# The last batch's second product as seven block products, with one block sum made by two accumulating DMAs

## The chip, the core and the metric

The kernel runs on one core of one Trainium2 chip. Its time is the device time of one execution in microseconds, taken as the median of several runs. The profile is one further execution with the hardware profiler on; its span runs from the first to the last instruction and is shorter than the device time of that execution.

## What is computed

Two stages. The first is attention between 512 tokens and 32 states of each of 8 batches and 8 heads, in both directions; the second takes the result, rearranged to 8 x 544 rows of 512, through a two-layer net. Softmax is along the last axis.

```python
# x: (8, 8, 512, 64)   state: (8, 8, 32, 64)   scale = 1 / 8
a     = softmax(scale * x @ state.T)      # tokens read states
xread = a @ state
a2    = softmax(scale * state @ x.T)      # states read tokens
sread = a2 @ x
X = concat([xread, sread], tokens)        # -> (8 * 544, 512)
h = X @ w_in                              # w_in (512, 2048)
g = s * relu(h) ** 2 + b
return g @ w_out                          # w_out (2048, 512), result float32
```

## The kernel before

**The two layers.** `w_in` and `w_out` stay in SBUF as fp16 (`w_out16`: four tiles of four row blocks). For tokens the state's values are folded into `w_in` first (`at_M`: M = state @ w_in for each head), so that layer one of a batch is M times the attention weights A (`layer1_x`, 16 blocks f of 128 hidden units for 512 tokens). ScalarE takes the relu from PSUM into `r` (two f to a tile, five tiles), VectorE squares two f at a time into the batch's tile `g` of [128, 16 f, 512 tokens] (`square`, L397). The factor s and the bias b leave the hidden layer: s is applied at the end, and b becomes a row `bias_bc` that is added at the end.

**Layer two.** `layer2(tag, rr, q)` (L423) is a quarter of the sum over f for 128 tokens: four matmuls, each with a 128 x 128 block of g as the loaded operand and `w_out_f(f)` of 512 columns streaming past it, into one PSUM bank. There are two such banks (`ps_o`, tag `po`). After four quarters `store` (L435) makes s * ops + bias in one VectorE instruction (L437) and sends the 128 rows out by DMAs on SP's queue (L441).

**The order.** It is written by hand; each engine works through its own queue in the order of the program. `phase(tag, before, behind)` (L573) runs 16 steps. A step issues the pieces due before it, then layer one of block i of the next batch, then at even steps the square of the blocks i-2 and i-1, then the pieces due behind. Batch b's phase runs layer one of batch b+1 beside layer two of batch b, from `l2(b)`: one quarter in each step. Attention for later batches, its loads on GpSimd's queue (`load_x`, `load_xn`) and the products M lie in the same steps. The last phase has the tag `sr`: layer one of the 256 state rows of all batches (`layer1_sr`, four matmuls of 256 columns in each step) beside layer two of batch 7. Layer two of the state rows follows it, in two blocks of 128 rows, the second in two column halves (L702, L706, L709).

Of the kernel before, what the change touches and what calls it, by code (L numbers as in the profile page):

```python
# [10 lines left out]
FP32 = mybir.dt.float32  # L11
FP16 = mybir.dt.float16
# [3 lines left out]
def kernel(  # L16
# [12 lines left out]
    nc = tc.nc  # L29
    AF = mybir.ActivationFunctionType  # L30
    ALU = mybir.AluOpType
    AX = mybir.AxisListType

    B, H, S, D = x.shape
    Ns = state.shape[2]
    DM = H * D
    DF = moe_w_in.shape[1]
    P = 128
    NK = DM // P
    NKF = DF // P  # L40
    NG = H // 4
    SCH = S // P
# [4 lines left out]
    HALF = S // 2  # L47
    scale = float(1.0 / np.sqrt(D))

    out_BSn = out.rearrange("(bb st) n -> bb st n", bb=B)  # L50

    konst = ctx.enter_context(tc.tile_pool(name="konst", bufs=1))
    wpool = ctx.enter_context(tc.tile_pool(name="wpool", bufs=1))
# [6 lines left out]
    opool = ctx.enter_context(tc.tile_pool(name="opool", bufs=4))  # L60
# [3 lines left out]
    ps_o = ctx.enter_context(tc.tile_pool(name="ps_o", bufs=2, space=bass.MemoryType.PSUM))  # L64
    ctx.enter_context(tc.manual_schedule())

    def two_banks(name, dtype=FP32, own=False):

        pool, tag = (ps_t, "pt") if own else (ps_a, "pa")
        return pool.tile([P, 2, 2048 // mybir.dt.size(dtype)], dtype, name=name, tag=tag)  # L70

    def mm(out, lhsT, rhs, start=True, stop=True, tp=None, is_transpose=None):
        skip = out.offset * mybir.dt.size(out.dtype) >= 2048
        return nc.tensor.matmul(  # L74
            out, lhsT, rhs, start=start, stop=stop, tile_position=tp,
            is_transpose=is_transpose, skip_group_check=skip,
        )
# [21 lines left out]
    s_bc, b_bc = sb_bc[:, 0:1], sb_bc[:, 1:2]  # L99
# [3 lines left out]
    bias_bc = konst.tile([P, DM], FP32, name="bias_bc")  # L103
    srdT = konst.tile([P, NK, Ns, B], FP16, name="srdT")
    w_in16 = [wpool.tile([P, NK, 512], FP16, name=f"w_in16_{j}") for j in range(NJ)]
    w_out16 = [wpool.tile([P, 4, DM], FP16, name=f"w_out16_{q}") for q in range(NKF // 4)]


    xh_t, xn_t = {}, {}
# [1 line left out]
    def load_x(b):  # L111

        if b > 2:
            nc.gpsimd.tensor_copy(ahead, at[b - 1]["xT"][0:1, 0, 0])  # L114
        xh_t[b] = xpool.tile([P, NG, NT, D], FP16, name=f"xh_{b}", tag="xh")
        for g in range(NG if b else 1):
            nc.gpsimd.dma_start(  # L117
                out=xh_t[b][:, g].rearrange("p j d -> p (j d)"),
                in_=x[b, 4 * g : 4 * g + 4].rearrange("r (t j) d -> (r t) (j d)", j=NT),
            )  # L120

    def load_xn(b):

        xn_t[b] = xpool.tile([P, H, SCH, D], FP16, name=f"xn_{b}", tag="xn")
        for jh in range(4):
            nc.gpsimd.dma_start(  # L126
                out=xn_t[b][32 * jh : 32 * jh + 32].rearrange("t h c d -> t h (c d)"),
                in_=x[b].rearrange("h (t jh c) d -> jh t h (c d)", t=32, jh=4)[jh],
            )
# [5 lines left out]

    def load_w_out(q):
        nc.gpsimd.dma_start(
            w_out16[q], moe_w_out.rearrange("(q f p) n -> q p f n", p=P, f=4)[q]
        )

    rows = state.rearrange("b (g r) n d -> (r n) (b g) d", g=NG)
# [12 lines left out]
    load_w_in(1)  # L154
    load_x(1)
    load_w_out(0)
    load_w_in(2)
    load_w_out(1)
# [7 lines left out]
        return w_in16[f // 4][:, k, P * (f % 4) : P * (f % 4) + P]  # L166

    def w_out_f(f):
        return w_out16[f // 4][:, f % 4, :]


    def place(h):
# [24 lines left out]
    def pair_states(i0, i1):  # L197
        nc.vector.transpose(
            stE[:, i0:i1].rearrange("p i n e -> p (i n e)").bitcast(FP32),
            stn[:, i0:i1].rearrange("p i d -> p (i d)").bitcast(FP32),  # L200
        )
# [26 lines left out]
    def at_xT(b, g=None, p=None):  # L228

        if "xT" not in at[b]:  # L230
            keep = b < 3
            at[b]["xT"] = (konst if keep else apool).tile(
                [P, NG, S, 2], FP16, name=f"xT_{b}", tag=f"xTk{b}" if keep else "xT"
            )
        out = at[b]["xT"].rearrange("p g s e -> p g (s e)").bitcast(FP32)
        in_ = xh_t[b].rearrange("p g j d -> p g (j d)").bitcast(FP32)
        nc.vector.transpose(part(out, p, g), part(in_, p, g))  # L237
# [141 lines left out]
    G_t, R_t = {}, {}  # L379
# [43 lines left out]
    def layer2(tag, rr, q):  # L423
        if q == 0:
            ops_t[tag, rr] = ps_o.tile([P, DM], FP32, name=f"ops_{tag}_{rr}", tag="po")
        for f in range(4 * q, 4 * q + 4):
            nc.tensor.matmul(  # L427
                ops_t[tag, rr],
                G_t[tag][:, f, P * rr : P * rr + P],
                w_out_f(f),  # L430
                start=(f == 0),
                stop=(f == NKF - 1),
            )

    def store(tag, rr, rows, n=1):  # L435
        osb = opool.tile([P, DM], FP32, name=f"osb_{tag}_{rr}", tag="osb")
        nc.vector.scalar_tensor_tensor(  # L437
            osb, ops_t.pop((tag, rr)), s_bc, bias_bc, ALU.mult, ALU.add
        )
        for i in range(n):  # L440
            nc.sync.dma_start(rows[i], osb[P // n * i : P // n * i + P // n])  # L441

    def out_x(b, rr):
        rows = out_BSn[b, 0:S]
        if b:
            store(b, rr, rows.rearrange("(t r i e) n -> r i t e n", r=SCH, i=2, e=2)[rr], 2)
        else:
            store(b, rr, [rows.rearrange("(t r j) n -> r j t n", r=SCH, j=4)[rr]])

    def spread_scalars():  # L450
        sps = two_banks("sbps")[:, 0, 0:2]
        mm(sps, ones32, sb_one)
        act(sb_bc, sps)
# [174 lines left out]
    def first():  # L628

        out = []  # L630
        units = [(rr, 3) for rr in (0, 1)]
        units += [(rr, q) for rr in (2, 3) for q in range(4)]
        out += [(1, bias_all)]
        for n, (rr, q) in enumerate(units):
            step = n + n // 2
            out += [(step, lambda rr=rr, q=q: layer2(0, rr, q))]
            if q == 3:
                out += [(step + 1, lambda rr=rr: out_x(0, rr))]
        return out

    def l2(b, lead=0):

        out = []
        for i in range(NKF):
            step = max(0, (i - lead) * NKF // (NKF - lead))
            if i and i % 4 == 0:
                out += [(step, lambda i=i: out_x(b, i // 4 - 1))]
            out += [(step, lambda i=i: layer2(b, i // 4, i % 4))]
        return out[:lead], out[lead:]

    left = []
    for b in range(0, B):
        before, behind = l2(b, 3 if b == 1 else 0) if b else ([], first())
        behind = left + behind
        if b + 3 < B:
            before += [(2 if b else 5, lambda b=b: load_x(b + 3))]
        if b + 3 < B:
            before += [(13, lambda b=b: at_xT(b + 3))]
        if b and b + 2 < B:
            before += [(7, lambda b=b: load_xn(b + 2))]  # L660
        if b == B - 3:
            before += [(9, lambda: load_xn(0))]
        if b == B - 2:
            before += [(4, lambda: load_xn(1)), (7, lambda: load_xn(2))]
        if b == 0:
            before += [(4, lambda: pair_states(4, NR)), (3, lambda: turn_states(4, 12, act)), (4, lambda: turn_states(12, NR, act))]
        if b + 2 < B:
            s = (1, 2, 3, 3, 4, 4, 5, 6, 7, 8, 9) if b else (5, 6, 7, 8, 9, 8, 9, 10, 11, 12, 13)
            before += [] if b else [(3, lambda: at_xT(2))]
            before += chain(b + 2, s)  # L670
            if b:
                before += [(7, lambda b=b: at_a2(b + 2))]
                before += [(10, lambda b=b: at_a2T(b + 2, dve))]
        if b > 1 and b + 1 < B:
            before += [(3 if b == B - 2 else 1, lambda b=b: at_V(b + 1))]
        if b:
            plan = [(6 if b < B - 2 else 0, 1, [(b + 1, 3), (b + 2, 0)][: B - 1 - b])]
            plan += [(12, 1, [(b + 2, 1), (b + 2, 2)])] if b + 2 < B else []
            plan += [(1, 1, [(2, 2)])] if b == 1 else []
        else:  # L680
            plan = [(2, 0, [(1, 3)]), (10, 0, [(2, 0), (2, 1)])]
        for step, own, units in plan:
            make, copies, left = pieces(step, own, *units)
            before, behind = before + make, behind + copies
        if b == B - 2:
            before += late(0, (1, 2, 3, 4, 5, 6, 7)) + late(1, (5, 6, 7, 7, 8, 9, 10))
            before += late(2, (8, 9, 10, 11, 12, 13, 15))
        phase(b + 1 if b + 1 < B else "sr", before, behind)
        if b:
            out_x(b, 3)  # L690


# [6 lines left out]
    for part in range(2):  # L699
        sl = slice(DM // 2 * part, DM // 2 * part + DM // 2)  # L700
        for f in range(NKF):
            nc.tensor.matmul(  # L702
                ops[:, sl], G_t["sr"][:, f, P:], w_out_f(f)[:, sl],
                start=(f == 0), stop=(f == NKF - 1),
# [35 lines left out]
```

## Time and profile before

| | us |
|---|---|
| time, median of 3 runs (lowest to highest) | 233.09 (233.02 to 233.31) |
| the profiled execution, own time | 233.29 |
| its span | 231.5 |
| last phase (`sr`), first matmul to the first of the state rows' layer two | 198.85 to 219.65 |
| one square, 128 x 1024 fp16 (L397), mean | 0.683 |
| one eviction of a layer-two bank (L437), mean | 0.745 |
| a store of 128 KB on SP (L441), issue to landing, median | 2.6 |
| a load xn of 128 KB on GpSimd's queue (L126), issue to landing, median | 6.1 |
| granted TensorE clock, mean over the span | 0.989 |

How to read it: the chain of waits goes back from the last instruction to what released each step. The order of time lists instructions with their start and length, merged where alike, and in square brackets how long the engine had stood idle before them and what ended it. The answer by stretches gives busy time and, in brackets, number of instructions for each engine, then the granted clock, the share of the DMA engines' time and GB/s. PE is TensorE, PEld its loading of weights, DVE VectorE, ACT ScalarE, POOL GpSimd, SP the engine that issues stores.

### The profile page before, as it was taken

How to read it: one execution, taken by the hardware profiler on the slowest of the kernel's cores; microseconds unless marked ns; L12 is line 12 of the kernel's file. 1: busy time of each engine (PE TensorE's matmuls, PEld its weight loads, DVE VectorE, ACT ScalarE, POOL GpSimd, SP SyncE). 2: the span in 40 equal slices, each digit the busy share in tenths (PEclk: the TensorE clock that was granted, in tenths of full speed). 3: DMA queues.
4: the chain of work that ended last, by engine and by line, in shares of the span. 5: the costliest groups of instructions: out<-in, count | busy, mean ns of one | idle time of the engine just before them, and what ended most of it. 6: DMA issues, size and time to landing. Idle time of an engine off the chain costs nothing.

```text
span 231.5 us, 4326 instructions
## 1 busy us (share of the span) xinstructions
PE 219.7 (95%) x1735; PEld 101.7 (44%) x1735; DVE 164.0 (71%) x251; ACT 130.5 (56%) x247; POOL 34.7 (15%) x65
## 2 busy tenths in 40 slices
PE   6687999999999999999999999999999999999993
PEld 2143334344444444444444444444434444665552
DVE  2887998788997699759884988498736686422330
ACT  2285676583886568646855685568477445323200
POOL 8431001006002300320025200030003120000000
PEclk9799999999999999999999999999999999999998
DMA  7999990625932960494149923182223782132222
GB/s 168 197 204 207 208 127 14 149 68 86 171 64 53 127 121 19 99 134 91 41 93 135 186 47 76 44 111 45 56 43 61 117 139 45 31 64 46 47 60 76
DMA packets 22920, 22.40 MB, mean 97 GB/s; under 512 B 4084, under 2 KB 16628, under 8 KB 22900
## 3 DMA queue, kind: packets, MB, share of 16 engines
q0 software_dynamic: 16640, 12.52, 37.3%
q1 hardware_dynamic: 5584, 9.44, 16.7%
q8 instruction: 13, 0.21, 0.3%
q10 hardware_dynamic: 676, 0.16, 0.3%
q14 instruction: 7, 0.06, 0.1%
HBM read 25.72 MB, written 8.91 MB: 150 GB/s over the span
## 4 chain that ended last, share of the span: by engine, by line
PE 84%; DMA 7%; DVE 3%; ACT 2%; POOL 2%; issue 1%; ACTq 0%; POOLq 0%
PE ops L427 45%; PE hps L389 22%; DMA w_in<-in_moe_w_in_dram 7%; PE mps L74 4%; PE hps_sr L389 3%; PE T L74 3%; PE vps L74 2%; PE ops_sr L702 2%; PE aps L74 2%; PE ops_sr L427 1%; POOL xh L117 1%; POOL w_in L132 1%; ACT E L316 1%; DVE g L416 1%; DVE U L257 1%
## 5 line engine op out<-in xcount | busy, mean ns | idle before, releaser
L427 PE MATMUL ops<-w_out,g 128*128 128x512 f16 x512 | 130.7, 379 | 0.7 <-DMA w_out<-in_moe_w_out_dram 0.7
L392 ACT ACTIVATE r<-hps 128x512 f16<-128x512 f32 x120 | 70.7, 600 | 48.1 <-PE hps L389 47.6
L427 PEld LDWEIGHTS <-g 128*128 128x128 f16 x512 | 50.0, 98 | 57.5 <-issue 0.9
L389 PE MATMUL hps<-A,M 128*128 128x512 f16 x240 | 70.1, 380 | 0.2 <-ACT r L392 0.2
L397 DVE TENSOR_TENSOR g<-r 128x1024 f16<-128x1024 f16 x60 | 40.9, 683 | 17.2 <-ACT r L392 17.0
L389 PEld LDWEIGHTS <-M 128*128 128x128 f16 x240 | 20.6, 97 | 27.9 <-issue 8.0
L372 ACT CAST M<-mps 128x512 f16<-128x512 f32 x50 | 29.4, 587 | 0.0
L126 POOL DMA_DIRECT2D xn<-in_x_dram x32 | 18.4, 585 | 54.5 <-PE vps L74 53.5
L437 DVE SCALAR_TENSOR_TENSOR osb<-ops,sb_bc,bias_bc 128x512 f32<-128x512 f32 x32 | 23.8, 745 | 1.1 <-PE ops L427 1.0
L316 ACT ACTIVATE E<-T,nms 128x512 f16<-128x512 f32 x16 | 11.0, 687 | 7.7 <-DVE nms L311 7.7
L392 ACT ACTIVATE r_sr<-hps_sr 128x256 f16<-128x256 f32 x16 | 6.1, 384 | 14.4 <-PE hps_sr L389 14.4
L114 POOL COPY ahead<-xT 1x2 f16<-1x2 f16 x5 | 0.9, 174 | 88.9 <-DVE xT L237 88.9
L274 ACT ACTIVATE E<-Dm 128x1024 f16<-128x1024 f32 (+1 forms) x9 | 8.7, 962 | 9.7 <-DVE Dm L267 9.6
L397 DVE TENSOR_TENSOR g_sr<-r_sr 128x512 f16<-128x512 f16 x8 | 3.4, 424 | 13.9 <-ACT r_sr L392 13.9
L257 DVE STREAM_TRANSPOSE U<-T 128x1024 f32<-128x1024 f32 (+1 forms) x9 | 10.9, 1207 | 3.0 <-PE T L74 3.0
L74 PE MATMUL mps<-w_in,stT 64*32 64x512 f16 x256 | 11.1, 388 | 1.3 <-DMA w_in<-in_moe_w_in_dram 1.3
L279 DVE TENSOR_REDUCE z<-E 128x32 f32<-128x1024 f16 (+1 forms) x9 | 9.9, 1100 | 2.8 <-ACT E L274 2.6
L354 DVE CAST srdT<-vps 128x128 f16<-128x128 f32 x8 | 5.8, 728 | 7.4 <-PE vps L74 7.4
L237 DVE STREAM_TRANSPOSE xT<-xh 128x1024 f32<-128x1024 f32 (+2 forms) x12 | 10.2, 870 | 1.0 <-DMA xh<-in_x_dram 1.0
L308 DVE TENSOR_REDUCE nm<-T 128x2 f32<-128x1024 f32 x8 | 9.7, 1214 | 1.2 <-PE T L74 1.2
L74 PE MATMUL T<-xT,stE 32*32 32x512 f16 (+1 forms) x192 | 7.5, 380 | 2.7 <-DVE xT L237 2.4
L267 DVE TENSOR_TENSOR Dm<-U,mu 128x1024 f32<-128x1024 f32 (+1 forms) x9 | 9.9, 1098 | 0.1
(59 smaller groups left out, 159.8 us busy)
## 6 DMA issues: line engine op xcount, KB each, us to landing
out_dram<-osb SPq DMA_DIRECT2D x56, 128.0 KB, 2.6
xn<-in_x_dram POOLq DMA_DIRECT2D x32, 128.0 KB, 6.1
xh<-in_x_dram POOLq DMA_DIRECT2D x15, 256.0 KB, 5.0
w_in<-in_moe_w_in_dram POOLq DMA_DIRECT2D x4, 512.0 KB, 12.5
w_out<-in_moe_w_out_dram POOLq DMA_DIRECT2D x4, 512.0 KB, 17.7
out_dram<-osb SPq DMA_DIRECT2D x4, 256.0 KB
xf<-in_x_dram SPq DMA_DIRECT2D x1, 512.0 KB, 3.5
out_dram<-osb_sr SPq DMA_DIRECT2D x1, 256.0 KB, 2.8
```

The source lines that it names most:

```text
L74: return nc.tensor.matmul(out, lhsT, rhs, start=start, stop=stop, tile_position=tp, is_transpose=is_transpose, skip_group_check=skip,)
L126: nc.gpsimd.dma_start(out=xn_t[b][32 * jh : 32 * jh + 32].rearrange("t h c d -> t h (c d)"), in_=x[b].rearrange("h (t jh c) d -> jh t h (c ...
L237: nc.vector.transpose(part(out, p, g), part(in_, p, g))
L257: nc.vector.transpose(part(U, p, g), part(at[b]["T"], p, g))
L267: nc.vector.tensor_tensor(blk(part(Dm, p, g)), blk(part(at[b]["U"], p, g)), over_n(part(at[b]["mu"], p, g)), ALU.subtract,)
L316: nc.scalar.activation(E2[:, g], at[b]["T"][:, g], AF.Exp, bias=at[b]["nms"][:, g : g + 1], scale=scale, accum_out=rs[:, g : g + 1],)
L372: nc.scalar.copy(at[b]["M"][:, g, 512 * j : 512 * j + 512], at[b]["mps", j][:, g, :])
L389: nc.tensor.matmul(hps, lhsT, rhs, start=(i == 0), stop=(i == len(terms) - 1))
L392: nc.scalar.activation(R_t[tag, f - f % 2][:, f % 2], hps, AF.Relu)
L397: nc.vector.tensor_mul(new_G(tag, r.shape[2])[:, f : f + 2], r, r)
L427: nc.tensor.matmul(ops_t[tag, rr], G_t[tag][:, f, P * rr : P * rr + P], w_out_f(f), start=(f == 0), stop=(f == NKF - 1),)
L437: nc.vector.scalar_tensor_tensor(osb, ops_t.pop((tag, rr)), s_bc, bias_bc, ALU.mult, ALU.add)
```

## The change

Layer two of batch 7 is a product of 512 tokens x 2048 hidden units with 2048 x 512 weights. It is cut into 2 x 2 blocks: A(i, j) is token half i and the even (j = 0) or odd (j = 1) blocks f of g, B(j, n) the same f and column half n of `w_out`. `fast_layer2` makes the four blocks of the result from seven products by Winograd's form of Strassen's scheme:

- sums of g: S1 = A10 + A11, S2 = S1 - A00, S3 = A00 - A10, S4 = A01 - S2;
- sums of the weights: T1 = B01 - B00, T2 = B11 - T1, T3 = B11 - B01, T4 = B10 - T2;
- products in this order: X = A00·B00, Y = A01·B10, X += S2·T2, W = S1·T1, X += S3·T3, W += S4·B11, X += A11·T4, with evictions of X, Y and W in between that put the four result blocks together in SBUF.

Each product is made in two units h (the blocks f below 8, and the others) of eight matmuls of 256 columns. Units 0 to 7 are due at steps 0 to 7, units 8 to 13 at steps 9 to 14. Each sum of g is made in two halves too. S3 gets a tile of its own. S2 and S4 are written by VectorE over A00 and A01. S1 is written over A10, once S3 has read it, by a DMA from SBUF to SBUF on GpSimd's queue that adds A11 to it (`s1`): two DMAs of 128 partitions x 4 rows of 256 fp16. X, Y and W are PSUM tiles of the tag `po`; Y and W follow one another.

The eight halves of weight sums are subtractions on VectorE at steps 14 and 15 of the phases of batches 2 to 5. `w_out16` becomes one tile. The results of batch 7 gather in two tiles `osx` and leave in eight DMAs, four at step 13 and four at step 15, in place of two after every fourth step.

```diff
+    def weight_sum(name, h):
+        if name not in fast_w:
+            fast_w[name] = konst.tile([P, NKF // 2, HALF], FP16, name=f"w_{name}")
...
+        nc.vector.tensor_sub(T[name], a, b)
+
+    def fast_layer2(b):
+        G = G_t[b]
+        S3 = konst.tile([P, NKF // 2, HALF], FP16, name="S3")
...
+        def A(i, j, h=None):
+            k0, k1 = (0, NKF // 2) if h is None else (4 * h, 4 * h + 4)
+            return G[:, 2 * k0 + j : 2 * k1 : 2, HALF * i : HALF * i + HALF]
...
+        def s3(h):
+            add(S3[:, 4 * h : 4 * h + 4], A(0, 0, h), A(1, 0, h), ALU.subtract)
+        def s1(h):
+            nc.gpsimd.dma_start(out=A(1, 0, h), in_=A(1, 1, h), accum_op=ALU.add)
+        def s2(h):
+            add(A(0, 0, h), A(1, 0, h), A(0, 0, h), ALU.subtract)
+        def s4(h):
+            add(A(0, 1, h), A(0, 1, h), A(0, 0, h), ALU.subtract)
...
+        products = [
+            ("X", A(0, 0), orig(0, 0), True, False),
+            ("Y", A(0, 1), orig(1, 0), True, True),
+            ("X", A(0, 0), summed("T2"), False, False),
+            ("W", A(1, 0), summed("T1"), True, False),
+            ("X", S3, summed("T3"), False, False),
+            ("W", A(0, 1), orig(1, 1), False, True),
+            ("X", A(1, 1), summed("T4"), False, True),
+        ]
+        out = [(u + u // 8, lambda u=u: product(*products[u // 2], u % 2)) for u in range(14)]
+        out += [(1, lambda: evict(top, 0, "X"))]
+        for h in range(2):
+            out += [(h, lambda h=h: s3(h)), (h, lambda h=h: s1(h))]
+            out += [(2 + h, lambda h=h: s2(h)), (4 + h, lambda h=h: s4(h))]
+        out += [
+            (3, lambda: evict(top, 0, "Y", True)),
+            (5, lambda: evict(top, 1, "X")),
+            (7, lambda: evict(low, 1, "W")),
+            (10, lambda: evict(low, 1, "X", True)),
+            (12, lambda: evict(top, 1, "W", True)),
+            (13, lambda: put(0, 0)), (13, lambda: put(0, 1)),
+            (15, lambda: evict(low, 0, "X")),
+            (15, lambda: put(1, 0)), (15, lambda: put(1, 1)),
+        ]
+        return out
...
-        before, behind = l2(b, 3 if b == 1 else 0) if b else ([], first())
+        if b == B - 1:
+            before, behind = [], fast_layer2(b)
+        else:
+            before, behind = l2(b, 3 if b == 1 else 0) if b else ([], first())
+        if 1 < b < 6:
+            name = f"T{b - 1}"
+            before += [(14 + h, lambda h=h, name=name: weight_sum(name, h)) for h in range(2)]
...
-        if b:
+        if b and b < B - 1:
             out_x(b, 3)
```

More of the change, by code (lines that the diff above doesn't have):

```diff
@@ L70, in two_banks, with mm @@
         return pool.tile([P, 2, 2048 // mybir.dt.size(dtype)], dtype, name=name, tag=tag)
-    def mm(out, lhsT, rhs, start=True, stop=True, tp=None, is_transpose=None):
-        skip = out.offset * mybir.dt.size(out.dtype) >= 2048
+    def mm(out, lhsT, rhs, start=True, stop=True, tp=None, is_transpose=None, skip=False):
+        skip = skip or out.offset * mybir.dt.size(out.dtype) >= 2048
         return nc.tensor.matmul(
@@ L105 @@
     w_in16 = [wpool.tile([P, NK, 512], FP16, name=f"w_in16_{j}") for j in range(NJ)]
-    w_out16 = [wpool.tile([P, 4, DM], FP16, name=f"w_out16_{q}") for q in range(NKF // 4)]
+    w_out16 = wpool.tile([P, NKF, DM], FP16, name="w_out16")
     xh_t, xn_t = {}, {}
@@ L137, in load_w_out @@
         nc.gpsimd.dma_start(
-            w_out16[q], moe_w_out.rearrange("(q f p) n -> q p f n", p=P, f=4)[q]
+            w_out16[:, 4 * q : 4 * q + 4], moe_w_out.rearrange("(q f p) n -> q p f n", p=P, f=4)[q]
         )
@@ L168, in w_out_f @@
     def w_out_f(f):
-        return w_out16[f // 4][:, f % 4, :]
+        return w_out16[:, f, :]
     def place(h):
@@ L448, in out_x @@
             store(b, rr, [rows.rearrange("(t r j) n -> r j t n", r=SCH, j=4)[rr]])
+    fast_w = {}
+    def weight_sum(name, h):
+        if name not in fast_w:
+            fast_w[name] = konst.tile([P, NKF // 2, HALF], FP16, name=f"w_{name}")
+        w = w_out16[:, 8 * h : 8 * h + 8]
+        B = [[w[:, k::2, HALF * n : HALF * n + HALF] for n in range(2)] for k in range(2)]
+        T = {k: t[:, 4 * h : 4 * h + 4] for k, t in fast_w.items()}
+        a, b = {
+            "T1": lambda: (B[0][1], B[0][0]),
+            "T2": lambda: (B[1][1], T["T1"]),
+            "T3": lambda: (B[1][1], B[0][1]),
+            "T4": lambda: (B[1][0], T["T2"]),
+        }[name]()
+        nc.vector.tensor_sub(T[name], a, b)
@@ new lines, in fast_layer2, with add, product, orig @@
+    def fast_layer2(b):
+        G = G_t[b]
+        S3 = konst.tile([P, NKF // 2, HALF], FP16, name="S3")
+        top, low = (opool.tile([P, 2, DM], FP32, name=f"osx_{b}_{i}", tag=f"osx{i}", bufs=1) for i in range(2))
+        ps = {}
+        def A(i, j, h=None):
+            k0, k1 = (0, NKF // 2) if h is None else (4 * h, 4 * h + 4)
+            return G[:, 2 * k0 + j : 2 * k1 : 2, HALF * i : HALF * i + HALF]
+        def add(out, x, y, op):
+            nc.vector.tensor_tensor(out, x, y, op)
+        def s3(h):
[6 more added lines that the diff above has]
+            add(A(0, 1, h), A(0, 1, h), A(0, 0, h), ALU.subtract)
+        def product(bank, lhs, rhs, first, last, h):
+            if first and h == 0:
+                ps[bank] = ps_o.tile([P, 2, HALF], FP32, name=f"opf_{b}_{bank}", tag="po")
+            for k in range(4 * h, 4 * h + 4):
+                for rr in range(2):
+                    mm(
+                        ps[bank][:, rr], lhs[:, k, P * rr : P * rr + P], rhs(k),
+                        start=(first and k == 0 and rr == 0), stop=(last and k == NKF // 2 - 1 and rr == 1), skip=True,
+                    )
+        def orig(j, n):
+            return lambda k: w_out_f(2 * k + j)[:, HALF * n : HALF * n + HALF]
+        def summed(name):
+            return lambda k: fast_w[name][:, k]
+        def evict(out, n, bank, plus=None):
+            out = out[:, :, HALF * n : HALF * n + HALF]
+            bias = bias_bc[:, HALF * n : HALF * n + HALF].unsqueeze(1).to_broadcast([P, 2, HALF])
+            nc.vector.scalar_tensor_tensor(
+                out, ps[bank], s_bc, bias if plus is None else out, ALU.mult, ALU.add
+            )
+        def put(i, rr):
+            t = (top, low)[i][:, rr]
+            rows = out_BSn[b, 0:S].rearrange("(t r i e) n -> r i t e n", r=SCH, i=2, e=2)[2 * i + rr]
+            for n in range(2):
+                nc.sync.dma_start(rows[n], t[64 * n : 64 * n + 64])
+        products = [
[23 more added lines that the diff above has]
+        return out
```

## The prediction

> **What bounds the kernel now.** I read the page first (busy shares, the chain that ended last, the costliest groups), then the order of time around the place of the change, then that stretch's busy time by engine, then the DMA rows. The page:
>
> ```profile
> span 231.5 us, 4326 instructions
> PE 219.7 (95%) x1735; PEld 101.7 (44%) x1735; DVE 164.0 (71%) x251; ACT 130.5 (56%) x247; POOL 34.7 (15%) x65
> ...
> PE 84%; DMA 7%; DVE 3%; ACT 2%; POOL 2%; issue 1%; ACTq 0%; POOLq 0%
> ...
> L427 PE MATMUL ops<-w_out,g 128*128 128x512 f16 x512 | 130.7, 379 | 0.7 <-DMA w_out<-in_moe_w_out_dram 0.7
> ```
>
> TensorE is busy 95% of the span and is 84% of the chain; the second product (L427) has 0.7 us of idle before it in all. So a multiplication taken away counts in full, and so does a wait put on TensorE. The 379 ns is one matmul's way through the array, not its price: that comes from starts in the order of time. The place is the stretch in which the states' first product runs beside the last batch's second product:
>
> ```profile
> 198.82 0.69 DVE L397 TENSOR_TENSOR g<-r 128x1024 f16<-128x1024 f16 x1 [0.43 <-ACT r L392]
> 198.85 0.60 PE L389 MATMUL hps_sr<-srdT,w_in 128*128 128x256 f16 x4
> ...
> 199.29 1.03 PE L427 MATMUL ops<-w_out,g 128*128 128x512 f16 x4
> 199.43 0.74 DVE L437 SCALAR_TENSOR_TENSOR osb<-ops,sb_bc,bias_bc 128x512 f32<-128x512 f32 x1
> ...
> 200.16 0.60 PE L389 MATMUL hps_sr<-srdT,w_in 128*128 128x256 f16 x4
> ...
> 219.65 3.62 PE L427 MATMUL ops_sr<-w_out,g_sr 128*128 128x512 f16 x16
> ```
>
> Sixteen steps fill 198.85 to 219.65, 20.80 us, 1.30 each: four matmuls of 256 columns (198.85 to 199.29, 0.44) and four of 512 (0.86). Thus 512 columns cost 216 ns and 256 columns 108 to 110. In the answer by stretches, whose columns are PE, PEld, DVE, ACT and POOL busy, then clock:
>
> ```profile
> 198.85:219.65 20.80, 20.80 (x129) 12.52 (x128) 6.79 (x13) 6.14 (x16) 0.00 (x0) 1.00 0.24 52
> ```
>
> TensorE has no gap there, the granted clock is 1.00, VectorE works 6.79 us of 20.80 and GpSimd nothing.
>
> **What is taken away.** The 64 matmuls of 512 columns become 7 products of 16 matmuls of 256: 14 units of eight (8 x 108 ns = 0.86 us) in place of 16 groups of four (0.86). Steps 8 and 15 have no unit, so 2 x 0.86 = 1.73 us go. The weight loads rise from 64 to 112, but the hps_sr matmuls, each with its own 128x128 load and only 256 columns, keep the 108 ns, so I price the extra loads at nothing; by the slower 110 ns of the last product's row (16 in 1.76 us) the gain is 1.5.
>
> **The weight sums.** Eight subtractions of 128x1024 fp16, two in each of four earlier phases, at steps 14 and 15. Nearest row: the squares, 0.69 us for 128x1024 fp16, 5.5 us in all. What hides them is VectorE's idle time at just that place, alike in each phase:
>
> ```profile
> 118.74 1.24 DVE L237 STREAM_TRANSPOSE xT<-xh 128x1024 f32<-128x1024 f32 x1
> 120.72 0.69 DVE L397 TENSOR_TENSOR g<-r 128x1024 f16<-128x1024 f16 x1 [0.75 <-ACT r L392]
> 123.31 0.69 DVE L397 TENSOR_TENSOR g<-r 128x1024 f16<-128x1024 f16 x1 [1.90 <-ACT r L392]
> ...
> 126.06 0.73 DVE L354 CAST srdT<-vps 128x128 f16<-128x128 f32 x1 [1.39 <-PE vps L74]
> ```
>
> Idle 0.75, 1.90 and 1.39 us before three instructions in a row: both fit. Price 0; without that cover the squares would come 1.4 us late, and the product that reads them only runs three steps (4 us) later. One w_out tile in place of four changes no transfer; I cost it at nothing, as parts of a tile are waited for separately elsewhere (M, g and srdT are written and read by parts).
>
> **The new wait.** In the last stretch VectorE gets six block sums (0.69 each) and seven evictions instead of four (0.74 each); 6.79 grows to about 13 of 19 us, so not its load but its order counts. Unit 5 (the second half of S2·T2) needs s2(1); that needs the second accumulating DMA; that needs s3(1), which reads the old block; and s3(1) stands in VectorE's queue behind the first eviction, which waits for unit 1. By rows:
> - Unit 1 is the second group: it starts at 200.59 and ends at 201.46. Eviction 201.50 to 202.24; s3(1) from 202.18 (neighbours overlap by 0.06) to 202.87; GpSimd issues at 202.93. The first DMA: s3(0) follows the osb eviction (199.43+0.74) from 200.10 to 200.79, issue at 200.85.
> - Undisturbed, unit 4 would start at 204.49 and unit 5 at 205.79.
> - After the landing: 0.05 to start, s2(1) 0.69, 0.05 to TensorE = 0.79.
>
> **The accumulating DMA is in no row.** Each moves 128 x 4 rows of 512 B. The nearest transfer is xn: fp32 read, fp16 written, in rows of 512 B, from the same queue. In a quiet window of 10 us:
>
> ```profile
> q0 software_dynamic: 1088, 0.52, 41.4%
> ...
> xn<-in_x_dram POOLq DMA_DIRECT2D x4, 128.0 KB, 3.8
> ```
>
> 1024 row packets (and 64 small ones) take 41.4% of 16 engines x 10 us: 61 ns each, 16 per engine and DMA, 0.96 us. The fastest landing of one xn is 3.0:
>
> ```profile
> DMA to landing us min/median/max: 3.0/6.1/9.4
> ```
>
> So about 2.04 us is fixed; with 512 rows the issue itself is 0.17 longer (w_in's issues 0.745, xn's 0.576): 2.2. Each new DMA has 32 packets per engine: landing = 2.2 + 32p, and the second queues behind the first, not before 200.85 + 2.2 + 64p. The price p has two ends. Below: 60 ns, as xn, which also reads 1024 B for 512 written. Above: 120, a packet's whole time twice, since source and destination both must be read. I take 82: one xn packet, plus 22 ns for a second read, the time of that queue's 4-byte packets in the trace. xn is the nearest row in packet length and queue, so the value stays near that end.
> - p = 82: first landing 205.67, second max(207.75, 208.30) = 208.30; unit 5 at 209.09, late by 3.30. Unit 4, at 206.46, has taken 1.97 of that.
> - p = 60: second landing 207.05; unit 5 late by 2.05.
> - p = 120: 210.73; late by 5.73.
>
> The Trainium skill (DMA: Bandwidth & Descriptors, "Anatomy of one DMA — SWDGE (gpsimd) path") fits a GpSimd-issued DMA by 2.0 us plus bytes at 436 GB/s, which is 2.6 us here; the sum by it would be a gain of 1.2. This trace's xn, half that size, never lands under 3.0. The skill's page Collectives: The Full Stack ("The bandwidth ceiling") says against the change that an add in the DMA path halves the rate, as it needs two source reads; by it p is near 120. No run here shows an accumulating one yet.
>
> **What is late next.** Behind the waiting s2(0) and s2(1) in VectorE's queue stand the eviction of Y, squares of the states' product, s4 and evict(top,1,X). With the landing at 208.30: s2(1) ends 209.04, Y's eviction 209.7, square 210.1, s4(0) and s4(1) 211.4, X's eviction 212.1. Unit 6, which takes Y's PSUM slot, comes at 210.4, unit 8, which writes X again, at 213.4: both behind their evictions. The squares held up are two of five r buffers, so ScalarE runs on. No second stall. **The stores** of the last batch, eight of 128 KB on SP, bunch: four at step 13, four at step 15, the latter issued about 221.6 instead of two at 220.6; by the 2.6 us row (out from osb) and 0.6 us of engine time for each further one, they land by 226.0, before the last two stores are issued (from 225.57 + 1.57 = 227.1). Cost 0; were the DMAs still full then, the last landing would be late by up to 1 us.
>
> **Sum:** 3.30 - 1.73 = +1.57 us on a span of 231.5, 233.1. The profiled execution took 233.29 (1.8 around its span), 0.2 above the median 233.09; against the median, 234.6.
>
> **Rivals.**
> - *The DMAs land early* (the other side). One mechanism: the second landing against 206.73, which is 3.8 us after its issue; before that the kernel gains. With xn's fastest 3.0: 205.93, unit 5 late by 0.93, -0.80: 232.3. For it: both ends in SBUF, engines 24% busy, no x loads left. Against: twice xn's rows, 32 x 60 ns more than fill the 1.0 us that 3.0 leaves. The skill's 2.6 would put it lower still, at 231.9.
> - *xn's own price*, p = 60: +0.3, 233.4, not to be told from no change.
> - *A double read at full price*, p = 120: +4.0, 237.1. For it: two operands, one written back. Against: xn's packets also read double bytes.
> - *Sums at one element per cycle.* The squares have one input twice; s3 and s2 have two. At the 1.29 us of the At row (128x1024 f16) in place of 0.69, s3(0), s3(1) and s2(1) are each 0.6 later and the total is +2.8: 235.9. Against: At has an fp32 factor with a broadcast; all is fp16 here.
>
> That the products would not shrink is excluded by the widths in the code.
>
> **Chances.** Forecast (p about 70 to 100) 0.36, with its own range 233.6 to 235.9; double read 0.24; early landing 0.22; p = 60 0.12; slow sums 0.06. A change of 0.2% is 0.47 us, about what can be measured here. Faster: early landing less its edge, 0.20; same: p = 60 and that edge, 0.14; slower: 0.66. The range 232.2 to 237.6 runs from early landing to a double read with 0.5 to spare, and leaves out no delay at all (231.4) and slower DMAs.
>
> **What would show it.** 112 products of 256 columns and steps of 1.30 us; s2(0) and s2(1) on VectorE waiting for a DMA of g, second landing 5.4 us after issue; TensorE idle about 2.0 and 1.3 us before units 4 and 5, nowhere else; phases 3 to 6 as long as before. I am wrong if TensorE also waits in the phases with the weight sums, if unit 6 or 8 waits for an eviction, or if the issue of s1(1) is not near 202.9.

## The result, and the profile after

The changed kernel took 236.82 us, median of 4 runs (233.91 to 238.18), against 233.06 us before; the ratio is 1.012, 95% interval 1.0077 to 1.0163, so it is 1.2% slower. The highest run, at a lower clock, is not in the ratio, which compares the means of the others. A later set on another occasion (below) gave 234.49 us and a ratio of 1.0072 (1.0046 to 1.0098). The profiled execution took 236.94 us, span 235.2. Its page, in the lines that were shown of before:

```profile
span 235.2 us, 4436 instructions
...
PE 220.2 (94%) x1783; PEld 107.4 (46%) x1783; DVE 174.9 (74%) x268; ACT 130.5 (55%) x247; POOL 38.1 (16%) x67
...
PE 75%; DMA 9%; issue 7%; DVE 3%; POOL 3%; ACT 1%; POOLq 0%; DVEq 0%
...
L427 PE MATMUL ops<-w_out,g 128*128 128x512 f16 x448 | 114.3, 379 | 1.2 <-DMA w_out<-in_moe_w_out_dram 1.2
```

The second product has 64 wide matmuls fewer, and TensorE's share of the chain fell from 84% to 75%, with DMA and issue up. Where it went is one place, in the order of time of the changed kernel (start, length, engine, instruction, idle before). L480 is the block sums of g, L486 the accumulating DMAs, L74 the products:

```profile
201.40 1.32 POOL L486 DMA_DIRECT2D g<-g  x1 [13.81 <-DVE S L480]
...
203.64 1.29 POOL L486 DMA_DIRECT2D g<-g  x1 [0.91 <-DVE S L480]
...
204.41 0.60 PE L389 MATMUL hps_sr<-srdT,w_in 128*128 128x256 f16 x4
...
207.36 0.69 DVE L480 TENSOR_TENSOR g<-g 128x1024 f16<-128x1024 f16 x1 [3.69 <-DMA g<-g]
...
208.11 1.24 PE L74 MATMUL opf_X<-w_T,g 128*128 128x256 f16 x8 [3.10 <-DVE g L480]
208.45 0.69 DVE L480 TENSOR_TENSOR g<-g 128x1024 f16<-128x1024 f16 x1 [0.39 <-DMA g<-g]
...
209.14 1.06 PE L389 MATMUL hps_sr<-srdT,w_in 128*128 128x256 f16 x4
...
209.99 1.92 PE L74 MATMUL opf_X<-w_T,g 128*128 128x256 f16 x8
...
211.70 0.87 PE L389 MATMUL hps_sr<-srdT,w_in 128*128 128x256 f16 x4
...
212.41 1.04 PE L74 MATMUL opf_W<-w_T,g 128*128 128x256 f16 x8
```

Read it by starts. The matmuls of step 4 start at 204.41 and take 0.44, so unit 4 was due at 204.85; it starts at 208.11, 3.26 us late, because s2(0) on VectorE waited for the first DMA. Then the matmuls themselves are slow: unit 4 to the next group 1.03 (0.87 elsewhere), that group 0.85 (0.44), unit 5 1.71 (0.87), the group after it 0.71 (0.44): 1.68 us more. The answer by stretches (TensorE busy, granted clock, DMA share, GB/s) has the reason:

```profile
204.00:208.00 4.00, 1.01 (x10) 1.00 1.01 112
208.00:212.00 4.00, 3.89 (x22) 0.60 0.00 0
212.00:216.00 4.00, 4.00 (x37) 0.97 0.00 0
```

From 208 to 212 the granted clock is 0.60 in the mean. Read by half microseconds, it is still 1.00 up to 208.5, 0.83 in the next half, 0.50 from 209.0 to 212.0, 0.75 and then 1.00 again: it falls at 208.8, 0.7 us after the matmuls have resumed, and stays at half for 3.4 us, which is a loss of 1.7. The whole last phase, 199.16 to 223.32, takes 24.16 us against 20.80: 3.36 more. Added up: 3.26 of waiting + 1.68 of slow clock - 1.73 saved + 0.14 (14 steps of 1.31 in place of 1.30) = 3.35. The other 0.31 of the 3.7 us by which the span grew lies before the phase, which began at 198.85 before; a second profile of the same kernel, below, has that start at 198.38, so it belongs to the run and not to the change.

### The profile page after: what moved, and what is told of

Its sections match the earlier page's. It is cut to its first block, busy times and chain, and to the rows that moved or that the text cites. A ratio compares the mean times of both kernels' runs of the same rounds, so it can differ in the third digit from the quotient of the medians.

```text
span 235.2 us, 4436 instructions
## 1 busy us (share of the span) xinstructions
PE 220.2 (94%) x1783; PEld 107.4 (46%) x1783; DVE 174.9 (74%) x268; ACT 130.5 (55%) x247; POOL 38.1 (16%) x67
## 4 chain that ended last, share of the span: by engine, by line
PE 75%; DMA 9%; issue 7%; DVE 3%; POOL 3%; ACT 1%; POOLq 0%; DVEq 0%
PE ops L427 36%; PE hps L389 21%; DMA w_in<-in_moe_w_in_dram 7%; PE mps L74 3%; PE opf_X L74 3%; DMA g<-g 2%; PE hps_sr L389 2%; PE T L74 2%; PE vps L74 2%; PE ops_sr L807 2%; PE opf_W L74 1%; PE ops_sr L427 1%; PE aps L74 1%; POOL xn L126 1%; POOL xh L117 1%
## 5 line engine op out<-in xcount | busy, mean ns | idle before, releaser
L427 PE MATMUL ops<-w_out,g 128*128 128x512 f16 x448 | 114.3, 379 | 1.2 <-DMA w_out<-in_moe_w_out_dram 1.2
L427 PEld LDWEIGHTS <-g 128*128 128x128 f16 x448 | 43.8, 98 | 53.8 <-issue 1.4
L437 DVE SCALAR_TENSOR_TENSOR osb<-ops,sb_bc,bias_bc 128x512 f32<-128x512 f32 x28 | 20.8, 744 | 1.0 <-PE ops L427 1.0
L114 POOL COPY ahead<-xT 1x2 f16<-1x2 f16 x5 | 1.6, 327 | 88.4 <-DVE xT L237 88.4
L74 PE MATMUL mps<-w_in,stT 64*32 64x512 f16 x256 | 11.0, 383 | 1.7 <-DMA w_in<-in_moe_w_in_dram 1.7
L74 PEld LDWEIGHTS <-g 128*128 128x128 f16 x96 | 9.7, 102 | 4.9 <-DVE g L480 3.4
L389 PE MATMUL hps_sr<-srdT,w_in 128*128 128x256 f16 x64 | 10.2, 288 | 0.0
```

What stands on the lines that cost most here:

```text
L74: return nc.tensor.matmul(out, lhsT, rhs, start=start, stop=stop, tile_position=tp, is_transpose=is_transpose, skip_group_check=skip,)
L389: nc.tensor.matmul(hps, lhsT, rhs, start=(i == 0), stop=(i == len(terms) - 1))
L427: nc.tensor.matmul(ops_t[tag, rr], G_t[tag][:, f, P * rr : P * rr + P], w_out_f(f), start=(f == 0), stop=(f == NKF - 1),)
L437: nc.vector.scalar_tensor_tensor(osb, ops_t.pop((tag, rr)), s_bc, bias_bc, ALU.mult, ALU.add)
```

## The experiments

All times are medians; the kernel before, run beside them, took 232.99 (first four), 233.05 (next four) and 232.85 (last two).

| run | us (lowest to highest) | ratio to before, 95% interval |
|---|---|---|
| sum on VectorE | 231.6 (231.47 to 231.81) | 0.9942 (0.9925 to 0.9958) |
| matmuls in the gap | 234.5 (234.35 to 235.04) | 1.0071 (1.0054 to 1.0088) |
| other order of products | 231.91 (231.29 to 232.31) | 0.9952 (0.9933 to 0.997) |
| sum before eviction | 234.98 (233.98 to 235.66) | 1.0083 (1.006 to 1.0107) |
| weight sums alone | 233.03 (232.27 to 234.23) | 1.0001 (0.9982 to 1.0019) |
| copy without add | 233.35 (232.81 to 235.57) | 1.0024 (1.0002 to 1.0046) |
| first half on VectorE | 235.32 (233.35 to 235.93) | 1.0077 (1.0045 to 1.0109) |
| changed kernel again | 234.49 (233.79 to 235.92) | 1.0072 (1.0046 to 1.0098) |
| other order, own bank | 231.89 (231.64 to 232.44) | 0.996 (0.9945 to 0.9975) |
| first add twice | 240.99 (240.72 to 241.31) | 1.0346 (1.0322 to 1.037) |

**The sum on VectorE.** Undoes the DMAs alone.

```diff
-            nc.gpsimd.dma_start(out=A(1, 0, h), in_=A(1, 1, h), accum_op=ALU.add)
+            add(A(1, 0, h), A(1, 0, h), A(1, 1, h), ALU.add)
```

> The two accumulating DMAs are replaced by two VectorE additions of the same blocks (0.69 us each) at the same places; all else is the changed kernel. Theory A (the whole loss is the wait of unit 4 for the landing of the first DMA, and the slow clock behind it): the saving of 1.73 us stands alone, unit 4 waits at most 0.2 us, time 231.4 to 231.8. Rival B (the seven-product form itself loses, through VectorE's longer queue, the weight sums or the weight loads): time 233 or more.

231.6, in theory A's interval. The chain of waits of this run (start, length, what):

```profile
203.99 0.61 DVE g L480
204.60 0.05 issue
204.65 1.05 PE opf_X L74 x8
205.70 0.44 PE hps_sr L389 x4
206.13 0.87 PE opf_X L74 x8
```

The DMA is gone from the chain; units 4 and 5 follow each other at the full rate. The seven products, the weight sums, the evictions and the bunched stores are worth about 1.4 us of gain together (232.99 - 231.6); rival B falls. The 1.4 is the 1.73, less 0.14 for the steps of 1.31 and less 0.21 for which unit 4 still waits (the matmuls of its step start at 204.00 in this trace and take 0.44, unit 4 starts at 204.65).

**The weight sums alone.** Layer two of batch 7 goes back to `l2` and `out_x`; one tile `w_out16` and the eight sums stay, their results unused.

```diff
-        if b == B - 1:
-            before, behind = [], fast_layer2(b)
-        else:
-            before, behind = l2(b, 3 if b == 1 else 0) if b else ([], first())
+        before, behind = l2(b, 3 if b == 1 else 0) if b else ([], first())
```

> The kernel before with only the one w_out tile and the eight weight sums added (their results are not used); layer two of batch 7 as before. Theory A (they lie in VectorE's idle time at steps 14 and 15): within 0.3 us of the kernel before, 232.8 to 233.3, stretches of the middle phases as long as before. Rival B (squares come late and TensorE waits): 233.5 or more.

233.03 against 233.05: theory A. How they fit is seen on VectorE in the changed kernel, in the same place that was shown of before:

```profile
120.21 0.65 DVE L466 TENSOR_TENSOR w_T<-w_out,w_T 128x1024 f16<-128x1024 f16 x1
121.03 0.69 DVE L397 TENSOR_TENSOR g<-r 128x1024 f16<-128x1024 f16 x1 [0.17 <-ACT r L392]
121.64 0.68 DVE L466 TENSOR_TENSOR w_T<-w_out,w_T 128x1024 f16<-128x1024 f16 x1
123.62 0.69 DVE L397 TENSOR_TENSOR g<-r 128x1024 f16<-128x1024 f16 x1 [1.30 <-ACT r L392]
```

The idle 0.75 before the first square became 0.17, and the 1.90 before the second became 1.30; both squares still wait for ScalarE, so neither is late. Two different inputs take the same 0.65 to 0.69 us as a square.

**The changed kernel again.** No edit.

> The changed kernel itself, on the chip of the experiments. Theory A (two outcomes from run to run: the first landing 4.7 us after issue, TensorE idle about 2 and then 1.3 us, full clock, about 234 to 235; or a landing delayed by an instruction fetch on one DMA engine, idle over 3 us, a slow clock, 236.5 to 237): times of both kinds, 233.9 to 237, and a profile that has either the late landing and the slow clock or neither. Rival B (the loss is constant): all within 0.5 us of 236.8.

Times from 233.79 to 235.92, median 234.49: lower than the first set, not constant, so rival B falls. No run comes to 236.5, so of theory A's two kinds only the first is seen in this set. The profiled execution (234.37) is of the first kind; its TensorE in order of time:

```profile
206.20 1.05 PE L74 MATMUL opf_X<-w_T,g 128*128 128x256 f16 x8 [1.98 <-DVE g L480]
...
208.51 1.05 PE L74 MATMUL opf_X<-w_T,g 128*128 128x256 f16 x8 [0.83 <-DVE g L480]
```

and by stretches:

```profile
204.00:208.00 4.00, 1.71 (x15) 1.00 0.75 84
208.00:212.00 4.00, 3.49 (x32) 1.00 0.00 0
```

Two waits, 1.98 and 0.83, and full clock. The phase's first matmul is here at 198.38, so unit 5 was due at 198.38 + 0.44 + 5 x 1.31 = 205.37 and is 3.14 late. This is the loss with the first landing on time and at full clock. The two profiled executions are 2.57 us apart (236.94 and 234.37): 1.68 of it is the slow clock, 0.12 the waiting (3.26 against 3.14), and 0.78 the start of the phase (199.16 against 198.38), which lies ahead of the accumulating DMAs. The late landing thus added little by itself; it made one wait of 3.26 out of two of 2.14 and 1.00 (by starts), and behind that one the clock fell. The lines "DMA to landing" of the two profiles, the first set's and this one's:

```profile
DMA to landing us min/median/max: 4.7/5.3/5.9
```

```profile
DMA to landing us min/median/max: 4.7/4.8/4.8
```

The first landing is 5.9 us after its issue in the one, 4.8 in the other. In the packets' own records of the first profile 15 of the 16 DMA engines have done the first DMA by 205.3 and the sixteenth at 206.53; one instruction fetch of 16 KB runs from 205.12 to 206.07. In the second profile the fetch ran from 204.88 to 205.84 and the straggler is in the second DMA, which one engine ended at 207.40 and the other fifteen between 206.5 and 206.7. With the first half on VectorE the fetch was over (204.63) before the DMA's first packet (205.2), and no engine straggled. The records don't name the engine, so that fetch and straggler share one is inferred from the times of these profiles, not shown, and so is the fetch as the cause of the late landing.

**Matmuls in the gap.**

```diff
+        def keep_busy(n):
+            dps = two_banks("busy", own=True)[:, 0, :]
+            for _ in range(n):
+                nc.tensor.matmul(dps, ones16[:, :P], ones16, start=True, stop=True)
...
+        out = [(4, lambda: keep_busy(14))] + out
```

> The changed kernel with 14 matmuls of 512 columns (3.0 us, into an unused PSUM bank) put before unit 4, where TensorE waits for the DMA. They add work, but only inside the wait. Theory A (1.69 us of the loss is a lower clock that TensorE is given after the idle time): the matmuls after unit 4 keep 108 ns, no slice of the granted clock is under 9, time 235.0 to 235.4 or 1.5 us and more under the changed kernel's 236.8. Rival B (the matmuls after the wait are long for another reason, such as late evictions or r buffers): their lengths stay, time 236.7 or more.

234.5 with a spread of 0.7 us; 3.0 us of added work cost nothing, since it lies in a wait of 3.1: unit 4 starts at 207.83, later than without the fill, and unit 5 at 209.18 with no wait left. The clock is 1.00 from 200 to 216 and matmuls are 108 ns. But in this profile the first landing came 4.7 us after its issue, so the fill alone is not shown to have saved the clock here: the changed kernel has the same time when its landing is undisturbed. What speaks for the fill is only that none of its six runs is near 236.

**The first add twice.** This lengthens the wait (half of S1 is then A10 + 2 A11).

```diff
-            nc.gpsimd.dma_start(out=A(1, 0, h), in_=A(1, 1, h), accum_op=ALU.add)
+            for _ in range(2 - h):
+                nc.gpsimd.dma_start(out=A(1, 0, h), in_=A(1, 1, h), accum_op=ALU.add)
```

> The first half's accumulating DMA is issued twice, the second waiting for the landing of the first (so that half of S1 is A10 + 2 A11). Theory A (the landing is paid in full, and idle time well over 3 us lowers the clock): unit 4 waits 6 to 7 us, the granted clock behind it is 0.5 to 0.7 for some 3 us, matmuls of 256 columns then take about twice 108 ns, time 239.5 to 241.5. Rival B (the slow matmuls of the changed kernel's profile were an accident and not the idle time): the same wait, full clock, matmuls of 108 ns behind it.

240.99. Its TensorE in order of time, and by stretches:

```profile
212.10 1.89 PE L74 MATMUL opf_X<-w_T,g 128*128 128x256 f16 x8 [6.47 <-DVE g L480]
213.78 1.06 PE L389 MATMUL hps_sr<-srdT,w_in 128*128 128x256 f16 x4
214.64 1.79 PE L74 MATMUL opf_X<-w_T,g 128*128 128x256 f16 x8
216.27 0.60 PE L389 MATMUL hps_sr<-srdT,w_in 128*128 128x256 f16 x4
```

```profile
208.00:212.00 4.00, 0.00 (x0) 0.67 0.96 105
212.00:216.00 4.00, 3.90 (x19) 0.50 0.24 26
216.00:220.00 4.00, 4.00 (x38) 0.98 0.00 0
```

After 6.5 us of idle time the clock is 0.50, unit 4 takes 1.68 us from start to start (double), and the clock is back at 0.98 from 216 on. By half microseconds it falls at about 209.4, while no matmul has run for almost 4 us and none runs yet, and returns at about 216.2. So idle time lowers the clock: theory A. The DMAs beside it don't: with the matmuls in the gap the DMA engines were 1.00 busy from 204 to 208, and the clock stayed 1.00. The Trainium skill (TensorE: Matmul & The Clock Gate, "What's actually happening") has the clock halved after an idle window of about 3.4 us. The traces agree on the half and nearly on the length: a drop followed a gap of 3.3 us in the changed kernel's first profile, and gaps of 2.0 and 2.4 us were followed by full clock. In the clock records of the profiles here, each stretch of one granted clock that begins and ends inside the execution lasts 3.41 us or a whole multiple of it (3.41 at 0.50 in the first profile, 6.83 here). So what a gap of some 3 us does may depend on where it falls between these points; no run here tests that.

**A copy without the add** leaves the addition out, so that S1 is A11.

```diff
-            nc.gpsimd.dma_start(out=A(1, 0, h), in_=A(1, 1, h), accum_op=ALU.add)
+            nc.gpsimd.dma_start(out=A(1, 0, h), in_=A(1, 1, h))
```

> The two DMAs copy A11 over A10 without adding (so S1 is A11 and the addition is left out); same queue, rows and places. Theory A (the add makes the DMA dearer: a second read): the issue falls from 1.30 to about 0.75 us, a packet from 75 to 60 ns or less, the landing from 4.7 to about 3.7 us, unit 5 about 1 us earlier, time 233.3 to 233.8. Rival B (512 rows of 512 B cost this much whatever is done with them): issue, packet and time as in the run with matmuls in the gap, 234.4 to 235.

233.35, in theory A's interval; rival B falls. The DMA rows of the changed kernel's first profile and of the copy, each in a window of 13 us (packets, MB, share of 16 engines):

```profile
q0 software_dynamic: 1056, 0.52, 37.0%
```

```profile
q0 software_dynamic: 160, 0.52, 14.1%
```

37.0% of 16 x 13 us is 77.0 us of engine time for two accumulating DMAs, 2.4 us on each engine for one; less its 32 small packets of 22 ns, a row packet takes 74.5 ns. The copy's 14.1% is 0.9 us on each engine: it packs the same bytes into 128 packets. The issue on GpSimd takes 0.77 us in place of 1.30, and the landings come 3.5 and 3.8 us after issue. The accumulating DMA thus costs 0.5 us of issue and 1.5 us on each engine more than the copy of the same 256 KB. How much of that is a second read, and how much the eight times smaller packets, this run doesn't separate: the copy has no packet of 512 B to compare. Theory A's reason is therefore not shown.

**The first half on VectorE.**

```diff
+            if h == 0:
+                return add(A(1, 0, h), A(1, 0, h), A(1, 1, h), ALU.add)
             nc.gpsimd.dma_start(out=A(1, 0, h), in_=A(1, 1, h), accum_op=ALU.add)
```

> The first half of S1 is added by VectorE, the second by a DMA as in the changed kernel. Theory A (each half's wait is its own landing; the longest idle time of TensorE is then under 3 us and the clock stays): unit 4 on time, unit 5 late by 2.0 to 2.6 us (landing 4.3 to 4.7 after an issue at 203.6), granted clock full, time 233.4 to 234.2, and a narrow spread. Rival B (the second DMA is slow only because it queues behind the first): it lands under 3.5 us, time below 233.

The profiled execution (234.29, 0.1 above theory A's interval) has the waits that theory A names: landing 4.3 us after issue, unit 4 on time, and on TensorE

```profile
208.42 1.05 PE L74 MATMUL opf_X<-w_T,g 128*128 128x256 f16 x8 [2.44 <-DVE g L480]
```

at full clock. Rival B falls: one DMA alone still takes 4.3 us, 0.4 less than in the pair. But the median, 235.32, and the spread missed the expectation: four of nine runs lie between 233.35 and 234.29, five between 235.32 and 235.93. The upper group has no profile. A wait in one piece that is now and then long enough for a slow clock would do it; that is open.

**The sum before the eviction.** `(1, lambda: evict(top, 0, "X"))` moves behind the loop over h, ahead of Y's eviction.

```diff
-        out += [(1, lambda: evict(top, 0, "X"))]
         for h in range(2):
...
         out += [
+            (1, lambda: evict(top, 0, "X")),
             (3, lambda: evict(top, 0, "Y", True)),
```

> Only the order of step 1 on VectorE changes: s3(1) and with it the second DMA's issue come before the first eviction of X, which waits for unit 1. The issue moves from 203.6 to about 202.7. The prediction's account (the second landing decides, 3.3 us): the time falls by 0.5 to 0.8 us. Theory A (the first landing decides, since it comes at 207.3): no change that can be told, within 0.4 us; the two DMAs' packets only stand closer together.

234.98: below the first set's 236.82, above the 234.49 of the changed kernel in the next set, so the time decides for neither; by the ratios, 1.0083 and 1.0072, the two kernels can't be told apart. The profile says more: the first landing comes 4.7 us after its issue, the second 6.2, as it queues behind the first; s2(1) starts at 208.17 and unit 5, which waits for it, at 208.92. So the second landing decides here, as the prediction had it, and yet the order gains nothing. Counted from the phase's first matmul (198.87 here, 198.38 in the changed kernel again), the second issue is 1.4 us earlier (201.9 against 202.86), the second landing only 0.1 (208.1 against 207.7). An earlier issue gains little when the 16 DMA engines are already full of the first half.

**Another order of the products.** A11·T4, which needs no sum of g, runs third, into a tile Z in Y's bank; S2·T2 is due two steps later.

```diff
             ("Y", A(0, 1), orig(1, 0), True, True),
+            ("Z", A(1, 1), summed("T4"), True, True),
             ("X", A(0, 0), summed("T2"), False, False),
...
-            ("X", S3, summed("T3"), False, False),
+            ("X", S3, summed("T3"), False, True),
             ("W", A(0, 1), orig(1, 1), False, True),
-            ("X", A(1, 1), summed("T4"), False, True),
```

> DMAs kept, but the product A11.T4, which needs none of the DMAs' sums, runs third (in its own PSUM tile, one eviction more), so that S2.T2 is wanted two steps (2.6 us) later; S2 is taken at steps 4 and 5, and the first eviction of X stands behind s3(1). Theory A (only the distance between issue and first use counts): with landings 5.9 and 4.8 us after issue the first S2 unit waits at most 0.6 us, clock stays full, time 231.4 to 232.4. Rival B (the DMAs cost something beyond the wait, on VectorE, GpSimd or the stores): 233 or more.

231.91, theory A: with both DMAs kept, the kernel is faster than before. TensorE has one wait left, for the eviction of Y that clears Z's bank:

```profile
204.24 1.03 PE L74 MATMUL opf_Z<-w_T,g 128*128 128x256 f16 x8 [0.41 <-DVE osx L513]
```

**The other order with a bank of its own for Z**, the PSUM pair that is free in this phase.

```diff
+                if bank == "Z":
+                    ps[bank] = two_banks(f"opf_{b}_Z", own=True)[:, 0].rearrange("p (r n) -> p r n", n=HALF)
```

> The other order of the products, with A11.T4 in the PSUM pair that lies unused in this phase, so that it doesn't wait for the eviction of Y (0.4 us of waiting before it in the profile of the other order). Theory A (that wait was the whole difference to the 1.73 us): no wait of TensorE before any unit, time 231.2 to 231.6, as the sum on VectorE or better. Rival B (the S2 units wait for the landings once the eviction's wait is gone): 231.7 to 232.3.

231.89, rival B. The wait for the eviction is gone and a wait for the second landing, 6.3 us after its issue, takes its place:

```profile
208.53 1.05 PE L74 MATMUL opf_X<-w_T,g 128*128 128x256 f16 x8 [0.34 <-DVE g L480]
```

The lowest median of all is that of the sum on VectorE, 231.6 us, 0.6% under the kernel before; the two other orders, at 0.5% and 0.4%, can't be told from it by their intervals.

## Why the prediction came out as it did

The direction, the place and the wait were right, and the forecast of 234.6 agrees with the later set (234.49) and its profile. The first set's 236.8 lies within the range, but above the likeliest case's own, and that is luck: the range reached so far up for a packet price of 120 ns, and what filled it was a slow clock that the sum didn't have.

- **What is taken away, 1.73:** right. Steps of 1.31 us, two without a unit; with the DMAs undone 1.4 us of it arrive, and the rest is accounted for there.
- **Weight sums at 0, one tile at 0, the stores at 0:** right (233.03 against 233.05 for the first two; from the first matmul of the state rows' layer two to the end of the span 11.85 us before and 11.88 after, so the bunched stores delay nothing). Sums of two inputs at 0.65 to 0.69 us refute the rival of slow sums.
- **The accumulating DMA, p = 82 ns:** measured 74.5, nearest to the value taken; the rival at full double price, 120, falls, and so does the 60 of xn. The base was read a little low: 41.4% of 160 us less 64 packets of 22 ns is 63 ns for a row packet of xn, not 61, which would have made p 85 and the wait 0.2 longer. That a second read makes up the rest of the price is not shown. The issue, priced at 0.745 from w_in, is 1.30, and GpSimd began 0.3 us behind s3 where 0.06 was allowed. The errors have opposite signs, and the first landing, 4.82 us after issue by the forecast, is 4.7 to 4.8 where nothing disturbs it: in part luck. The second issue came 4.48 us after the phase's first matmul where 4.08 was forecast, which by the prediction's own signs speaks against it, and its landing 4.8 us after the issue where 5.4 was forecast; these largely cancel too.
- **The wait, 3.30 in two pieces of 1.97 and 1.33:** measured 3.14 in the second profile, by starts 2.14 and 1.00.
- **The bound from the Trainium skill:** 2.6 us by the fit of "Anatomy of one DMA — SWDGE (gpsimd) path" (DMA: Bandwidth & Descriptors) is not reached even by the plain copy, 3.5. The rule of the Trainium skill's page Collectives: The Full Stack ("The bandwidth ceiling"), that an add halves the rate by a second read, has the right sign; the engine time here rose 2.6 times (0.9 to 2.4 us), and the copy also went out in larger packets, so the rule itself is not tested.
- **"No second stall":** right for what it followed (evictions, r buffers and squares behind the wait are on time), and yet here the account was incomplete. It did not ask what a wait of 2 us does to TensorE's clock if it grows to 3.3, nor what else runs on the 16 DMA engines: in the first profile the first landing came 1.2 us late, the two waits became one, and the slow clock behind it added 1.68, a term that the sum leaves out.
- **The order of the halves:** the prediction had the second landing decide. So it is in the second profile; in the first the late first landing decided, and unit 5 did not wait for the second at all.
- **Early landing as the rival on the other side:** its break-even, the second landing 3.8 us after issue, is borne out by the plain copy: landings at 3.5 and 3.8 with the GpSimd issue 0.4 later than forecast gave 233.35, a ratio just above 1.

Open: why the first set had higher times than the second, and what the upper group of the first half on VectorE did. Only two executions of the changed kernel have a profile, so how often the late landing and the slow clock occur is not known, and the sets of experiments ran on different chips, which is not excluded as a reason.

## What to carry to other kernels

An operation handed to a DMA in the middle of a dependent chain is paid by its latency, issue to landing, and not by the engine time that it frees: here 4.7 us replaced 0.69 of VectorE, and the same DMAs cost at most about 0.3 us (231.9 against 231.6) once independent products stood between issue and use. When a forecast contains a wait on TensorE, price the wait at its disturbed length too, and ask whether it then gets near the idle time after which the clock falls. A filler of useless matmuls in such a wait cost nothing here, 3.0 us of it in 3.1 us of waiting; that it keeps the clock up is likely but not shown.

## What was not expected of the hardware

- A DMA issue on GpSimd with an add takes 1.30 us for 512 rows, a plain one of the same shape 0.77.
- A plain copy of 256 KB from SBUF to SBUF goes out as 64 packets of 4 KB where the accumulating DMA needs 512 of 512 B; 0.9 against 2.4 us on each engine.
- One instruction fetch of 16 KB lasts 0.93 to 1.17 us in these stretches. In the profiles where it ran beside the DMAs, one of the 16 DMA engines ended its share 0.6 to 1.3 us after the others, and the landing waited for that one; that the fetch is the reason is inferred.
- A gap of 3.3 us on TensorE was followed by 3.4 us at a granted clock of 0.50, which began 0.7 us after the matmuls had resumed and cost 1.68 us; gaps of 2.0 and 2.4 us were not.
